# Block-diagonal 64-row products for groups 4 to 11 in a fused DeltaNet and gated-MLP kernel, with a re-planned order of work

## The chip, the cores and the metric

The kernel runs on one NeuronCore of a Trainium2 chip. The metric is the device time of one execution in microseconds (us). The kernel before takes 633.71 us in the median of 3 runs (633.09 to 634.2).

A core has a matrix engine (TensorE, PE in the profile, with weight loads as PEld), a vector engine (VectorE, DVE), a scalar engine (ScalarE, ACT), a general one (GpSimd, POOL) and one that issues transfers (SyncE, SP). Each works through its own instructions in order. TensorE writes to PSUM, which has eight banks of 2 KB per partition; the other engines copy from there to SBUF.

## The reference

Two parts follow each other. The first is a delta rule with a state per head (4 batches, 8 heads, 768 steps, head size 48):

```
k_n = k / (norm(k) + 1e-6)
for t in range(768):
    y[t]  = q[t] @ state
    v_old = k_n[t] @ state
    state = state + beta[t] * outer(k_n[t], v[t] - v_old)
```

The second is a gated MLP over the 3072 tokens of y (384 wide, 1536 hidden): `(sigmoid(x @ w_gate) * (x @ w_val)) @ w_out`. All in float32.

## The kernel before

**The recurrence in chunks.** The 768 steps are cut into 12 groups of 64 tokens. Within a group the recurrence becomes a triangular system: the updates u solve `(1/gamma + strictly lower part of K K^T) u = v - K state`. All 32 pairs of batch and head are done at once; a 64-token block is held as two 32-token halves that lie on different partitions. Per group g these steps run, named here as the planner names them:

- `gram`: K K^T of the keys (32 products of 48 rows, 64 records in the trace, since a float32 product leaves two). The diagonal 32x32 blocks are copied to `G` (line 258), the corner blocks between the two halves to `L` (line 262).
- `n`, `h`, `T`: norms and the inverse of the 32x32 triangular blocks on VectorE, for two groups together (`norms`, `solve`), with a transpose into `mt` at the end (line 310). Groups 0 and 1 take a shorter way: `solve_pair` inverts 16x16 blocks and `joining` (`pz`, `pm`, lines 366 and around) builds the 32x32 inverses with products.
- `pk` (`rest`, line 384): K state. `less` (line 393) subtracts it from v on VectorE.
- `u.0`, `u.1`, `u.2` (`updates`): the inverse times the first half (line 414), the corner block times that result, accumulated onto `pk` (line 407), then, after a second `less`, the inverse times the second half (line 414). `keep_u` (lines 420, 422) copies the results into `su`, a quarter of the partitions at a time, since heads of different kinds go to different places. In each 128-row operand four 32-row products lie beside each other.
- `pp` with `masked` (lines 273, 278): the masked q K^T. `yy` (`rows`, lines 442 and 445): the outputs. `pd` (`advance`, line 469) and `s` (line 478): the new state. `pt`, `xh`, `xl` (lines 500, 507, 509): the outputs transposed and split into a high and a low part for the MLP.

The chain from one group to the next is `pk`, `less`, `u.0`, copies, `u.1`, `less`, `u.2`, copies, `yy`, `pd`, `s`.

**The MLP in tiles.** Groups form units: 0 and 1 alone (256 tokens, "narrow"), then pairs (512 tokens, "wide"). A unit goes through 12 slices of the hidden width; each slice is a `gate`, a `val` and an `out` product of nine records each (lines 521 and 557; a narrow unit has gate and val in one step). float32 precision comes from splitting weights and inputs into two parts and making three products. In between run the sigmoid, the product and the split (lines 526, 531, 536, 541). Units 0 and 1 alternate in runs of slices (`RUNS`), because their weights arrive and are unpacked (lines 153 to 176) while they work.

**The order of work.** Nothing is ordered by hand: `schedule()` is a planner that runs when the kernel is built. Every step is a task with an engine, a cost in ns, the tasks it follows, and tokens it takes and gives back (`aux` for four PSUM banks, `mt`, `row` and others for buffers). For each engine the planner picks, among the tasks that can start soonest (within `SLACK`), the one with the highest level: the longest chain of costs behind it, plus `URGENCY` by name, plus `LIFTS` by group for the names in `FIRST` or `CHAIN`. The result is a fixed order for each engine. Up to the first product tile, gaps on TensorE are filled with `warm` products (line 185). The planner counts TensorE's instructions in pages of 256; `SHIFTS` tiny products ahead of `pz0` (line 191) move where the pages end.

Of the kernel before, what the change touches and what calls it, by code (L numbers as in the profile page):

```python
# [26 lines left out]
N = S // C  # L27
# [25 lines left out]
RUNS = {0: (0, 6, 12), 1: (0, 9, 12)}  # L53
EPS = 1e-6
EARLY, FLIGHT, HUSH = 3, 2, 6
QUIET = "pm0"
# [3 lines left out]
def deltanet_gated_mlp(ctx: ExitStack, tc: tile.TileContext, kd, qd, kv, beta, words, out):  # L60
# [13 lines left out]
    mt = const.tile([128, 2, CP, 32], F32, name="mt")  # L74
# [7 lines left out]
    scratch = wk.tile([128, 3, CP, 32], F32, name="scratch", tag="xa0", bufs=1)  # L82
# [22 lines left out]
    def load_rows(g, part):  # L105

        st = state[g]
        st["kv"[part]] = wk.tile([128, CP, D], F32, name=f"{'kv'[part]}_{g}", tag="kv"[part], bufs=2)
        pairs = [(st["kv"[part]].rearrange("p c d -> p (c d)"), kv[g, :, part * CP * D:(part + 1) * CP * D])]
        if part and g % 2 == 0:  # L110
            st["beta"] = wk.tile([128, 32], F32, name=f"beta_{g}", tag="beta", bufs=2)
            pairs.append((st["beta"], beta[:, g // 2]))
        move(pairs)

    def constants():
# [8 lines left out]
        state[0]["X"] = X = wk.tile([128, 1056], F32, name="X_0", tag="xa1", bufs=1)  # L124
        nc.gpsimd.memset(X, 0.0)
        nc.gpsimd.memset(scratch[:, 0], 0.0)
# [115 lines left out]
    def gram(g):  # L242
# [5 lines left out]
        st["L"] = L = wk.tile([128, CP, 32], F32, name=f"L_{g}", tag="L", bufs=2)  # L248
# [7 lines left out]
        def block(e, n):  # L256
            lo, hi, o = ((0, 128, 0), (32, 64, 32), (96, 128, 32))[n]
            (nc.vector.tensor_copy if g < 2 and e else nc.scalar.copy)(out=G[lo:hi, :, e * J:(e + 1) * J], in_=pg[e][lo:hi, :, o:o + 32].rearrange("q p t -> q t p"))  # L258

        def corner(e, t):  # L260
            lo, o = t + 32 * e, 32 - 32 * e
            nc.scalar.copy(L[lo:lo + 32, e * J:(e + 1) * J], pg[e][lo:lo + 32, :, o:o + 32])
# [25 lines left out]
    def solve(g):  # L288
# [21 lines left out]
        nc.vector.transpose(mt.rearrange("q g c i -> q i c g"), X.rearrange("q i (c g) -> q i c g", g=2))  # L310
        yield

    def lower_left(g):

        a = scratch[:, 0]
        nc.scalar.activation(a[:, :, 0:16].rearrange("q c t -> q t c"), state[0]["G"][:, 0:16, :, g], AF.Copy, scale=under)
# [28 lines left out]
    def flipped(g):  # L345

        nc.vector.transpose(scratch[:, 1].rearrange("q c t -> q (c t)"), mt[:, g].rearrange("q c t -> q (c t)"))
# [5 lines left out]
    def joining(g, n):  # L353
# [8 lines left out]
        lhsT, rhs = (scratch[:, 0], mt[:, g]) if n == "pz" else (scratch[:, 1], scratch[:, 2])  # L362
        out, rhs = out[:, :, 16:], rhs[:, :, 16:]
        for c in range(CP):
            for r in range(0, 128, 32):
                last = nc.tensor.matmul(out=out[r:r + 32, c], lhsT=lhsT[r:r + 32, c], rhs=rhs[r:r + 32, c], start=True, stop=True)
# [4 lines left out]
    def keep_z(g):  # L371

        nc.scalar.copy(scratch[:, 2, :, 16:], state[g]["pz"][:, :, 16:])


    def rest(g):
# [4 lines left out]
        for j in range(J):  # L381
            for e, x in KINDS:
                r, t = 64 * e, tokens_at(e, x)
                nc.tensor.matmul(out=pk[e][t:t + 64, j], lhsT=kq[r:r + D, x, j], rhs=su[r:r + D, 2 if x else e, j],  # L384
                                 start=j == 0, stop=True, skip_group_check=True)
        if g:
            st["R"] = [None, None]

    def less(g, e, step):
        st = state[g]  # L390
        if st["R"][e] is None:
            st["R"][e] = wk.tile([128, J, D], F32, name=f"R_{g}_{e}", tag="row", bufs=2)
        nc.vector.tensor_tensor(out=st["R"][e], in0=st["v"][:, e * J:(e + 1) * J], in1=st["pk"][e], op=ALU.subtract)  # L393

    def updates(g, step):

        st = state[g]
        if g == 0 and "R" not in st:
            st["R"] = [st["v"][:, e * J:(e + 1) * J] for e in range(2)]
        R, L = st["R"], st["L"]  # L400

        at = {(e, x): [tokens_at(e, x) + 32 * (k ^ e) for k in range(2)] for e, x in KINDS}
        if step == 1:
            for j in range(J):
                for e, x in KINDS:
                    one, two = at[e, x]
                    nc.tensor.matmul(out=st["pk"][e][two:two + 32, j], lhsT=L[one:one + 32, e * J + j], rhs=su[one:one + 32, 3 if x else e, j],  # L407
                                     start=False, stop=True, skip_group_check=True)
            return
        st["pu"] = pu = [ps_aux.tile([128, J, D], F32, name=f"pu_{g}_{step}_{x}", tag="aux") for x in range(1 if g else 2)]  # L410
        for j in range(J):
            for e, x in KINDS:
                r = at[e, x][step // 2]
                nc.tensor.matmul(out=pu[0 if g else x][r:r + 32, j], lhsT=mt[r:r + 32, g % 2, e * J + j], rhs=R[e][r:r + 32, j], start=True, stop=True)  # L414

    def keep_u(g, step, e, x):

        r, pu = tokens_at(e, x) + 32 * ((step // 2) ^ e), state[g]["pu"]
        if g == 0 and x:
            nc.vector.tensor_copy(out=su[r:r + 32, 3 if x else e], in_=pu[1][r:r + 32])  # L420
        else:
            nc.scalar.copy(su[r:r + 32, 3 if x else e], pu[0][r:r + 32])  # L422
# [168 lines left out]
    SHIFTS = 5  # L591
# [23 lines left out]
    pools = dict(flight=EARLY, aux=4, gv=1, po=2, G=1, gp=1, mt=2, scratch=1, row=2, ys=1, sg=2, h=2, u=2, L=2, xa=0, xb=1, mq=2)  # L615
# [422 lines left out]
```

## Time and profile before

| | |
|---|---|
| median of 3 runs | 633.71 us |
| profiled execution, whole | 636.26 us |
| its span, first to last instruction | 634.5 us |
| granted TensorE clock, mean | 0.991 |
| first product tile (`gate0`) starts | 50.62 us |
| TensorE busy | 617.0 us |
| VectorE busy | 393.7 us |
| ScalarE busy | 255.9 us |
| GpSimd busy | 10.0 us |

The groups of instructions name a line, an engine, an operation, what is written and read, the shape and the count, then busy time, mean length of one in ns, and the idle time ahead of it. In the timeline a row merges neighbours of one kind: start, length, engine, line, operation, shape, count, and in brackets the idle time before it and what ended that. Matmuls overlap, so the length of a row of them reaches past the start of the next row.

### The profile page before, as it was taken

Reading aid. Unit: us, or ns where it says so; the run is one execution under the profiler, and the core shown is the slowest. Engines: PE = TensorE matmul, PEld = TensorE weight load, DVE = VectorE, ACT = ScalarE, POOL = GpSimd, SP = SyncE. Lnnn points to the kernel's source line nnn. Section 1 sums busy time; section 2 is a strip of 40 time slices with the busy share of each in tenths; the row PEclk is TensorE's granted clock in tenths of the full one; section 3 lists DMA queues with packets and bytes.
Section 4 is the critical chain, followed back from the end, with each engine's and each line's share of the span. In section 5 each row is a group of like instructions: output and inputs, shape, how many; then the busy total and the mean of one; then the engine's idle time right before and its main releaser. Section 6 shows DMA issues by size and latency. Waiting matters only on the chain.

```text
span 634.5 us, 20716 instructions
## 1 busy us (share of the span) xinstructions
PE 617.0 (97%) x9372; PEld 502.4 (79%) x9381; DVE 393.7 (62%) x876; ACT 255.9 (40%) x506; POOL 10.0 (2%) x25
## 2 busy tenths in 40 slices
PE   8878999999999999999999999999999999999997
PEld 5457899989887777788787877778888777888886
DVE  4887779996699652499544499753399744212222
ACT  4477995264521234722224621235521143221212
POOL 3000000000000000000000000000000000000000
PEclk9978999999999999999999999999999999999999
DMA  8867663004210131020041130021130000010001
GB/s 220 263 167 219 190 189 96 2 28 113 61 50 26 27 110 38 2 74 5 23 112 28 35 101 2 26 66 48 35 101 1 1 3 3 2 51 0 1 1 50
DMA packets 16216, 40.75 MB, mean 64 GB/s; under 512 B 2944, under 2 KB 3968, under 8 KB 16128
## 3 DMA queue, kind: packets, MB, share of 16 engines
q1 hardware_dynamic: 15920, 39.10, 21.3%
q8 instruction: 73, 1.20, 0.8%
q10 hardware_dynamic: 208, 0.33, 0.1%
q14 instruction: 15, 0.12, 0.1%
HBM read 34.70 MB, written 4.72 MB: 62 GB/s over the span
## 4 chain that ended last, share of the span: by engine, by line
PE 87%; ACT 5%; DVE 5%; issue 1%; DMA 1%; SPq 0%; ACTq 0%
PE gv_g L521 26%; PE po L557 22%; PE gv_v L521 20%; PE pu L414 3%; PE warm L185 3%; PE pk L384 2%; PE pp L273 2%; PE yy L442 2%; PE pg L254 2%; PE yy L445 2%; ACT G L258 1%; PE pd L469 1%; PE pt L500 1%; PE pk L407 1%; ACT w L172 1%
## 5 line engine op out<-in xcount | busy, mean ns | idle before, releaser
L521 PE MATMUL gv_g<-x,w 128*128 128x512 f32 (+1 forms) x756 | 167.3, 368 | 0.7 <-DVE x L509 0.6
L557 PE MATMUL po<-h,w 128*128 128x512 f32 (+1 forms) x756 | 167.5, 366 | 0.3 <-DVE h L541 0.2
L557 PEld LDWEIGHTS po<-h,w 128*128 128x128 f32 x756 | 127.1, 188 | 25.1 <-DVE h L541 0.7
L521 PEld LDWEIGHTS gv_g<-x,w 128*128 128x128 f32 x756 | 126.7, 190 | 24.8 <-DVE x L509 0.9
L521 PE MATMUL gv_v<-x,w 128*128 128x512 f32 x540 | 136.9, 397 | 0.0
L521 PEld LDWEIGHTS gv_v<-x,w 128*128 128x128 f32 x540 | 99.9, 188 | 23.4
L536 ACT CAST h<-sg 128x512 fp32r<-128x512 f32 (+1 forms) x84 | 47.0, 559 | 144.0 <-DVE sg L531 139.7
L531 DVE TENSOR_TENSOR sg<-sg,gv_v 128x512 f32<-128x512 f32 x60 | 41.2, 687 | 97.9 <-PE gv_v L521 97.5
L526 ACT ACTIVATE sg<-gv_g 128x512 f32<-128x512 f32 (+1 forms) x84 | 45.0, 536 | 123.7 <-PE gv_g L521 123.4
L541 DVE TENSOR_TENSOR h<-sg,h 128x512 fp32r<-128x512 f32 (+1 forms) x84 | 51.4, 611 | 44.4 <-ACT h L536 43.9
L422 ACT COPY su<-pu 32x384 f32<-32x384 f32 x92 | 43.3, 470 | 51.8 <-PE pu L414 50.5
L305 DVE TENSOR_TENSOR tmp<-X,gp 128x31 f32<-128x31 f32 (+15 forms) x155 | 52.9, 341 | 4.1
L308 DVE TENSOR_TENSOR X<-X,tmp 128x31 f32<-128x31 f32 (+15 forms) x155 | 52.9, 342 | 3.8
L278 DVE TENSOR_TENSOR kqp<-pp,pmask 64x512 f32<-64x512 f32 x48 | 32.3, 686 | 7.6 <-PE pp L273 7.0
L478 DVE TENSOR_TENSOR su<-su,pd 48x384 f32<-48x384 f32 x40 | 22.0, 551 | 20.3 <-PE pd L469 19.6
L258 ACT COPY G<-pg 32x256 f32<-32x256 f32 (+1 forms) x66 | 26.0, 393 | 10.9 <-PE pg L254 9.5
L521 PE MATMUL gv_g<-xx,w 128*128 128x256 f32 x216 | 28.3, 285 | 0.7 <-DVE sg L531 0.7
L521 PEld LDWEIGHTS gv_g<-xx,w 128*128 128x128 f32 x216 | 26.6, 191 | 1.2 <-DVE sg L531 0.9
L185 PE MATMUL warm<-zero 128*128 128x512 bf16 x83 | 23.2, 430 | 2.4 <-issue 1.3
L393 DVE TENSOR_TENSOR R<-v,pk 128x384 f32<-128x384 f32 x44 | 22.3, 550 | 4.7 <-PE pk L384 4.2
L509 DVE TENSOR_TENSOR x<-pt,x 128x384 fp32r<-128x384 f32 x22 | 11.7, 554 | 19.9 <-ACT x L507 19.8
L414 PEld LDWEIGHTS pu<-R,mt 32*32 32x32 f32 x1408 | 16.6, 105 | 6.2 <-issue 5.1
(98 smaller groups left out, 482.8 us busy)
## 6 DMA issues: line engine op xcount, KB each, us to landing
raw<-in_words_dram SPq DMA_DIRECT2D x36, 384.0 KB, 3.8
kqp<-in_qd_dram SPq DMA_DIRECT2D x24, 256.0 KB, 4.0
v<-in_kv_dram SPq DMA_DIRECT2D x12, 384.0 KB, 4.0
k<-in_kv_dram SPq DMA_DIRECT2D x12, 384.0 KB, 3.5
kqp<-in_kd_dram SPq DMA_DIRECT2D x23, 192.0 KB, 3.5
out_dram<-ot SPq DMA_DIRECT2D x14, 256.0 KB, 2.0
out_dram<-ot SPq DMA_DIRECT2D x7, 128.0 KB, 1.7
kqp<-in_kd_dram ACTq DMA_DIRECT2D x1, 192.0 KB, 4.5
```

The source lines that it names most:

```text
L185: nc.tensor.matmul(out=hot[0], lhsT=z.to_broadcast([128, 128]), rhs=z.to_broadcast([128, 512]), start=True, stop=True)
L258: (nc.vector.tensor_copy if g < 2 and e else nc.scalar.copy)(out=G[lo:hi, :, e * J:(e + 1) * J], in_=pg[e][lo:hi, :, o:o + 32].rearrange(" ...
L305: nc.vector.tensor_tensor(out=tmp, in0=X[:, j:32, j:j + 1].to_broadcast([128, n, j]), in1=gp[:, j:j + 1, 0:j].to_broadcast([128, n, j]), o ...
L308: nc.vector.tensor_tensor(out=X[:, j:32, 0:j], in0=X[:, j:32, 0:j], in1=tmp, op=ALU.add)
L414: nc.tensor.matmul(out=pu[0 if g else x][r:r + 32, j], lhsT=mt[r:r + 32, g % 2, e * J + j], rhs=R[e][r:r + 32, j], start=True, stop=True)
L422: nc.scalar.copy(su[r:r + 32, 3 if x else e], pu[0][r:r + 32])
L521: nc.tensor.matmul(out=pg, lhsT=parts[w, f][:, a, k * 128:(k + 1) * 128], rhs=x[b][:, k], start=(k == 0 and q == 0), stop=(k == KC - 1 and ...
L526: nc.scalar.activation(h, st["g", f], AF.Sigmoid)
L531: nc.vector.tensor_tensor(out=h, in0=h, in1=st["v", f], op=ALU.mult)
L536: nc.scalar.copy(hh[:, 0], st["sg", f])
L541: nc.vector.tensor_tensor(out=hh[:, 1], in0=st["sg", f], in1=hh[:, 0].bitcast(F32), op=ALU.subtract)
L557: nc.tensor.matmul(out=po[k], lhsT=parts["o", f][:, w, k * 128:(k + 1) * 128], rhs=hh[:, a], start=begins(p, f) and q == 0 and (p > 1 or k ...
```

## The change

Six things change together.

- **Inverse as a block-diagonal operand (groups 4 to 11, `WIDE`).** `mt` becomes the front of a larger tile `both`, in which each 32-column inverse block has a second column block beside it. The solve's transpose `T` writes the blocks of all rows into column block 0; ScalarE copies those of the second and fourth quarter of the partitions to column block 1 (`aside`), and GpSimd clears them in column block 0 (`blank`). Two 32x32 blocks then stand on the diagonal of a 64x64 operand, and an update step is 16 products of 64 rows instead of 32 of 32 rows. So that both halves meet the right rows, v and beta are reordered on the way in for these groups, `less` takes 32-row quarters from alternating banks, and a second set of rows is gathered by four ScalarE copies (`gather`) and one subtraction.
- **64-row step between the halves (all groups).** ScalarE copies the whole bank of first-half results to `uc` (`keep_all`); `across` multiplies with corner blocks that stand off the diagonal of a zeroed 64x64 operand (`corner_of`), 16 products into a bank of its own (`pl`), and `less_first` subtracts that from the rows in place. The copies into `su` are no longer ahead of it. `rest` is left out for group 0, whose state is zero.
- **The first join (`pz`) with 64 rows**: `lower_left` runs as four quarter instructions into a block-diagonal operand, and 32 products take the place of 64.
- **Seven tiles of group 0 first** (`RUNS`), instead of six.
- **Small steps held back**: where TensorE's last task was a product tile and groups 4 on are concerned, a task counts as startable only `HOLDS` after it is ready (`pp` 24 us, `pt` 15, `gram` 1), unless nothing else is left.
- **Planner tables**: costs, `URGENCY`, `LIFTS`, `SLACK`-like limits, `SHIFTS` from 5 to 32, a charge of 180 ns for a small step that follows a product tile in place of a discount of 200 for one that follows a small step; and the key rows for the state have one buffer instead of two.

```diff
-RUNS = {0: (0, 6, 12), 1: (0, 9, 12)}
+RUNS = {0: (0, 7, 12), 1: (0, 9, 12)}
+WIDE = 4
...
+    both = const.tile([128, 2, 2, J, 2, 32], F32, name="both")
+    flat = both.rearrange("p g s j h i -> p (g s j h i)")
+    mt = flat[:, 0:2 * CP * 32].rearrange("p (g c i) -> p g c i", g=2, c=CP)
+    corner_of = [const.tile([128, J, 2, 32], F32, name=f"L{i}") for i in range(2)]
...
+        to = both[:, :, :, :, 0].rearrange("q g s j i -> q i (s j) g") if g >= WIDE else mt.rearrange("q g c i -> q i c g")
+        nc.vector.transpose(to, X.rearrange("q i (c g) -> q i c g", g=2))
...
+    def aside(q):
+        nc.scalar.copy(both[32 * q:32 * q + 32, :, :, :, 1], both[32 * q:32 * q + 32, :, :, :, 0])
+    def blank(q):
+        nc.gpsimd.memset(both[32 * q:32 * q + 32, :, :, :, 0], 0.0)
+    def lower_left(g, q):
+        mine = slice(32 * q, 32 * q + 32)
+        nc.scalar.activation(wide_a[mine, :, q % 2, 0:16].rearrange("q c t -> q t c"), state[0]["G"][mine, 0:16, :, g], AF.Copy, scale=under[mine])
...
         for c in range(CP):
-            for r in range(0, 128, 32):
-                last = nc.tensor.matmul(out=out[r:r + 32, c], lhsT=lhsT[r:r + 32, c], rhs=rhs[r:r + 32, c], start=True, stop=True)
+            if n == "pz":
+                for r in (0, 64):
+                    last = nc.tensor.matmul(out=out[r:r + 64, c], lhsT=wide_a[r:r + 64, c], rhs=mt[r:r + 64, g, c, 16:], start=True, stop=True)
...
+    def gather(g, q):
+        nc.scalar.copy(st["pc"][rows], st["pk"][1 ^ q % 2][rows])
...
+    def less(g, s, q=None):
+        rows = slice(0, 128) if q is None else slice(32 * q, 32 * q + 32)
+        r, st = halves_of(g)[rows, s], state[g]
+        nc.vector.tensor_tensor(out=r, in0=r, in1=st["pk"][s] if g < WIDE else st["pc"] if q is None else st["pk"][s ^ q % 2][rows], op=ALU.subtract)
+    def less_first(g, s):
+        r = halves_of(g)[:, s]
+        nc.vector.tensor_tensor(out=r, in0=r, in1=state[g]["pl"], op=ALU.subtract)
...
+            if g >= WIDE:
+                for r in (0, 64):
+                    nc.tensor.matmul(out=pu[0][r:r + 64, j], lhsT=both[r:r + 64, g % 2, s, j], rhs=R[r:r + 64, s, j], start=True, stop=True)
+                continue
...
+    def keep_all(g):
+        nc.scalar.copy(uc, state[g]["pu", 0][0])
+    def across(g):
+                nc.tensor.matmul(out=pl[r:r + 64, j], lhsT=corner_of[g % 2][r:r + 64, j], rhs=st["uc"][r:r + 64, j], start=True, stop=True)
...
-    SHIFTS = 5
+    SHIFTS = 32
...
+                if e == PE and not shape[0] and not filling:
+                    options = [o for o in options if o[0] >= when[o[1]["n"]] + HOLDS.get(o[1]["name"].rstrip("0123456789."), 0) or int(o[1]["name"].strip("abcdefghijklmnopqrstuvwxyzU").split(".")[0]) < 4] or options
...
-    LIFTS = {0: 100000, 1: 15000, 2: 0, 3: 15000}
+    LIFTS = {0: 60000, 1: 15000, 2: -5000, 3: 5000}
...
-    TURNED = 200
+    SWITCH = 180
+    HOLDS = dict(gram=1000, pp=24000, pt=15000, pk=0, pd=0)
```

More of the change, by code (lines that the diff above doesn't have):

```diff
@@ L416, in keep_u, with halves_of @@
[L416 to L422, printed above, removed]
+                nc.tensor.matmul(out=pk[e][t:t + 64, j], lhsT=kq[r:r + D, x, j], rhs=su[r:r + D, 2 if x else e, j], start=True, stop=True)
+    def halves_of(g):
+        return state[g]["v"].rearrange("p (s j) d -> p s j d", s=2)
@@ L746, in keeps @@
             return out
-        task(f"u{g}.0", PE, 810, lambda: updates(g, 0), r + [f"T{g if g < 2 else g - g % 2}"], take=("aux",) * (2 if two else 1))
-        k0 = keeps(0, [f"u{g}.0"])
-        task(f"u{g}.1", PE, 810, lambda: updates(g, 1), k0 + corners[g] + r, free=("L",))
-        l1 = [task(f"less{g}.1.{e}", DVE, 555, lambda e=e: less(g, e, 1), [f"u{g}.1"], free=("aux",)) for e in range(2)]
-        task(f"u{g}.2", PE, 810, lambda: updates(g, 2), l1, take=("aux",) * (2 if two else 1), free=("row", "row", "mt") if g else ("mt",))
@@ L752, in recurrence @@
-        k2 = keeps(2, [f"u{g}.2"])
-        task(f"yy{g}", PE, 2150, lambda: rows(g), k2 + m + was, take=("aux", "aux", "ys"))
+        word, pay = ("U", 600) if g >= WIDE else ("u", 812)
+        task(f"{word}{g}.0", PE, pay, lambda: updates(g, 0), r[:4] + ([f"T{g if g < 2 else g - g % 2}"] if g < WIDE else blanks[g - g % 2]), take=("aux",))
+        task(f"uc{g}", ACT, 472, lambda: keep_all(g), [f"{word}{g}.0"], take=("uc",))
+        k0 = keeps(0, [f"{word}{g}.0", f"uc{g}"])
+        task(f"a{g}", PE, 600, lambda: across(g), [f"uc{g}"] + corners[g], take=("aux",), free=("L", "uc"))
@@ L754, in recurrence @@
+        kind = (1,) if g >= WIDE else (0, 1)
+        l2 = [task(f"less{g}.2.{k}", DVE, 555, lambda k=k: less_first(g, k), [f"a{g}"] + r, free=("aux",) if k else ()) for k in kind]
+        task(f"{word}{g}.2", PE, pay, lambda: updates(g, 1), l2, take=("aux",) * (2 if two else 1), free=("mt",))
+        k2 = keeps(1, [f"{word}{g}.2"])
+        task(f"yy{g}", PE, 2147, lambda: rows(g), k0 + k2 + m + was, take=("aux", "aux", "ys"))
         yc = [task(f"y{g}.{e}", DVE if two and e else ACT, 560 if two and e else 480, lambda e=e: keep_y(g, e), [f"yy{g}"], free=("aux",)) for e in range(2)]
@@ L949, in schedule @@
                 small = t["name"][:3] not in ("gat", "val", "out")
-                cost -= TURNED if small and shape[0] else 0
+                cost += SWITCH if small and not shape[0] and not filling else 0
                 shape[0] = small
```

175 lines of the change are left out of this document (98 added, 77 removed), and 13 rows, old and new, of the table URGENCY.

## Prediction, made before the result was known

> **What bounds the kernel now.** I read the page's busy shares first, then the busy time by stretch, then the timeline of TensorE (its rows: start us, length us, engine, line, operation, tiles, shapes, count, idle time before).
>
> ```profile
> span 634.5 us, 20716 instructions
> ...
> PE 617.0 (97%) x9372; PEld 502.4 (79%) x9381; DVE 393.7 (62%) x876; ACT 255.9 (40%) x506; POOL 10.0 (2%) x25
> ```
> ```profile
> 32.00:48.00 16.00, 12.30 (x447) 9.36 (x453) 13.67 (x21) 11.85 (x19) 0.00 (x0) 0.79 0.63 172
> ...
> 172.00:545.00 373.00, 373.00 (x5460) 297.38 (x5461) 239.89 (x543) 128.34 (x258) 2.91 (x3) 1.00 0.14 39
> ```
>
> From 172 to 545 us TensorE (first figure after the stretch) is never idle, at a granted clock of 1.00; VectorE has work for 239.89 and ScalarE for 128.34 of those 373 us. There a saved TensorE microsecond is a saved microsecond of the span, and added work on the other engines costs nothing while it is not late. Before 50 us it is the other way round: from 32 to 48 us VectorE is busy for 13.67 of 16, and TensorE partly idles or runs `warm` fillers.
>
> Lengths of matmul rows overlap, so I take a step's cost from one row's start to the next row's start.
>
> ```profile
> 194.92 0.94 PE L469 MATMUL pd<-su,k 64*48 64x48 f32 x64
> ...
> 204.28 2.26 PE L521 MATMUL gv_v<-x,w 128*128 128x512 f32 x9
> 206.38 2.26 PE L557 MATMUL po<-h,w 128*128 128x512 f32 x9
> 208.57 1.15 PE L384 MATMUL pk<-su,kqp 48*64 48x48 f32 x64
> 209.65 2.36 PE L521 MATMUL gv_g<-x,w 128*128 128x512 f32 x9
> 211.85 2.26 PE L557 MATMUL po<-h,w 128*128 128x512 f32 x9
> ...
> 216.14 0.88 PE L414 MATMUL pu<-R,mt 32*32 32x48 f32 x64
> 216.95 2.35 PE L521 MATMUL gv_g<-x,w 128*128 128x512 f32 x9
> 219.23 0.88 PE L407 MATMUL pk<-su,L 32*32 32x48 f32 x64
> 220.04 2.35 PE L521 MATMUL gv_v<-x,w 128*128 128x512 f32 x9
> ...
> 226.55 1.15 PE L442 MATMUL yy<-su,kqp 48*64 48x48 f32 x64
> 227.63 1.14 PE L445 MATMUL yy<-su,kqp 128*64 128x48 f32 x32
> 228.70 2.36 PE L521 MATMUL gv_g<-x,w 128*128 128x512 f32 x9
> ...
> 542.00 0.82 PE L500 MATMUL pt<-ident,ys 128*128 128x128 f32 x6
> ```
>
> A 32-row step (`updates`, 32 products, 64 records) holds TensorE from 216.14 to 216.95, 0.81 us or 12.7 ns a record; the corner product on line 407 also 0.81. `rest` takes 1.08 for 64 records (16.9 ns), the first half of `rows` 1.08 for 64 (16.9), `advance` 0.86 for 64 records with 48 weight columns (13.4), and the full-height half of `rows` 1.07 for 32 (33.4 ns). A product tile of nine records takes 2.10 (204.28 to 206.38), but 2.19 ahead of a small step and 2.20 behind it: going into a burst of small steps and out of it costs 0.19.
>
> **The change part by part.** *The 64-row step.* For groups 4 to 11 each of the three update products becomes 16 products of 64 rows by 64 columns, 32 records; for groups 0 to 3 only the middle one does (`across`). The trace has no such step with this exact pattern. The nearest row is `rows` line 442 (64 columns of weights, 48 moving, half heights taken in turn): 32 records at 16.9 ns are 0.54 us. Bounds: 13.4 ns as in `advance`, 0.43; and 33.4 ns as in the full-height half, 1.07, if the two halves did not run beside each other. I take 0.54, a saving of 0.27 a step. Outside the startup there are 8 groups x 3 + 3 groups x 1 = 27 of them: **-7.3 us** (bounds -10.3 and +7.0).
>
> ```profile
> L414 PEld LDWEIGHTS pu<-R,mt 32*32 32x32 f32 x1408 | 16.6, 105 | 6.2 <-issue 5.1 <-ACT L L262 0.4
> ...
> L442 PEld LDWEIGHTS yy<-su,kqp 64*64 64x64 f32 (+1 forms) x736 | 12.0, 134 | 4.0 <-issue 2.5 <-ACT L L262 0.7 <-DVE su L420 0.4
> ```
>
> In the groups by line a load of 32 columns takes 105 ns and one of 64 columns 134: 1.28 times, not twice. The Trainium skill, "TensorE: Matmul & The Clock Gate", section on LDWEIGHTS, says that a weight load costs its columns divided by 1.2 ns and nothing for its rows. By that rule 32 loads of 64 columns are worth 64 loads of 32, and this term would be 0 instead of -7.3.
>
> *The pair of joins.* `pz` falls from 64 products to 32. Group 1's runs from 49.43 to 50.62 (rows below), 1.19; with 64 records at 16.9 ns it is 1.08: **-0.1**. Group 0's lies in the startup.
>
> *Holding back.* With `HOLDS`, the planner lets `pp` wait up to 24 us, `pt` 15 and `gram` 1 after they are ready, for groups 4 on, unless another small step has just opened a burst. From 194.92 to 542.00 (rows above, the first and the last) I count 60 bursts; 48 contain a step of the recurrence (`pk`, `pu`, `yy`, `pd`) and stay; 12 hold nothing but `pp`, `pt` or `gram`. If 8 of the 12 join another burst, 8 x 0.19 = **-1.5** (bounds 0 and -2.3).
>
> *Startup.* The first product tile starts at 50.62.
>
> ```profile
> 34.70 0.54 PE L414 MATMUL pu<-v,mt 32*32 32x48 f32 x15 [0.74 <-DVE mt L351]
> 36.17 1.19 PE L414 MATMUL pu<-v,mt 32*32 32x48 f32 x49 [0.93 <-issue]
> 37.70 1.06 PE L185 MATMUL warm<-zero 128*128 128x512 bf16 x2 [0.34 <-issue]
> 38.69 1.09 PE L407 MATMUL pk<-su,L 32*32 32x48 f32 x64
> ...
> 49.43 1.26 PE L366 MATMUL pz<-mt,scratch 32*32 32x16 f32 x128
> 50.62 2.37 PE L521 MATMUL gv_g<-x,w 128*128 128x256 f32 x18
> ...
> 54.43 0.68 PE L384 MATMUL pk<-su,kqp 48*64 48x48 f32 x31 [0.79 <-issue]
> ...
> 59.53 0.79 PE L366 MATMUL pm<-scratch 32*32 32x16 f32 x49 [1.35 <-issue]
> 60.25 3.65 PE L521 MATMUL gv_g<-x,w 128*128 128x256 f32 x18
> ```
> ```profile
> 31.48 2.71 DVE L278 TENSOR_TENSOR kqp<-pp,pmask 64x512 f32<-64x512 f32 x4
> 34.22 0.42 DVE L351 TENSOR_TENSOR mt<-mt,pz 128x256 f32<-128x256 f32 x1
> ```
> ```profile
> 34.71 0.78 ACT L316 ACTIVATE scratch<-G,under 128x256 f32<-128x256 f32 x1
> 35.55 0.83 ACT L172 CAST w<-u 128x768 fp32r<-128x768 f32 x1
> 37.39 0.96 ACT L422 COPY su<-pu 32x384 f32<-32x384 f32 x2 [1.01 <-PE pu L414]
> ```
>
> Now the corner product (38.69) waits for four copies of quarters, two on ScalarE (37.39 to 38.35) and two on VectorE; after, for one copy of the whole bank, half of ScalarE's 0.96: -0.5 us. The corner product itself halves in records, 1.09 to about 0.6 at that stretch's clock of 0.79: -0.5. The removed `rest` of group 0 and 27 more tiny `shift` products stand where fillers stand: 0. Against it, `lower_left` becomes four instructions of about 0.78 instead of one, twice, so 2 x 3 x 0.78 = 4.7 us more of ScalarE, of which group 1's 2.3 fall beside weight preparation; ScalarE has 4.1 us free between 32 and 48, and if that cover is gone the chain is up to 2.3 late. Waits for nothing the profile names ("issue") cut into steps: 0.93 here; and VectorE ran 2.71 us of masks right before the operation (34.22) that the chain waited for, at a priority that the new table changes. I take -1 for these two of a possible -3.6: startup **-2.0** (bounds +2.3 and -4.6).
>
> *Early product tiles.* Seven tiles of group 0 instead of six ahead of group 1's nine: the same tiles in another order, 0. The waits at 54.43 and 59.53 (0.79, 1.35) and the tile at 60.25 that took 3.65 where the same work took 2.37 at 50.62 (+1.28) may come back elsewhere: 0, bounds -3.4 and +3.
>
> ```profile
> q8 instruction: 73, 1.20, 0.8%
> ```
>
> These waits look like instruction fetches: 1.20 MB in 73 packets is 16 KB, about 256 of TensorE's 18,753 loads and products, each. The change removes some 2,100 of them (28 steps x 64, 128 of `rest`, 2 x 128 of `pz`, less 54 of `shift`), 8 packets. The Trainium skill, "Runtime: NRT & Kernel Launch", section on instruction fetch, calls crossing such a block mostly hidden, which would make every such term 0; the trace shows 0.8 to 1.4 us at the worst ones.
>
> *Other engines.*
>
> ```profile
> 213.22 2.02 DVE L310 STREAM_TRANSPOSE mt<-X 128x1024 f32<-128x1024 f32 x1
> ```
> ```profile
> 217.09 1.95 ACT L422 COPY su<-pu 32x384 f32<-32x384 f32 x4 [4.38 <-PE pu L414]
> ```
> ```profile
> L286 POOL MEMSET X<- 128x1024 f32 x5 | 4.8, 963 | 449.2 <-DVE gp L199 449.2
> ```
> ```profile
> 357.12 1.02 DVE L509 TENSOR_TENSOR x<-pt,x 128x384 fp32r<-128x384 f32 x2 [3.36 <-ACT x L507]
> ```
> ```profile
> 364.15 1.10 PE L521 MATMUL gv_g<-x,w 128*128 128x512 f32 x4
> ```
>
> Between the transpose that ends a pair's solve (213.22 to 215.24) and the first update (216.14) now stand two ScalarE copies of 1,024 elements (estimated from 0.83 for 768: 1.1 each) and a GpSimd clear (0.96): about 3.2 us later, once a pair. Each group's chain has two more subtractions (half of 1.02 each) ahead of its first update and four gathering copies (1.95) beside it, but one copy instead of four (-1.46) and one subtraction less behind it: about even. Work queued behind them on ScalarE (the product tiles' sigmoid and split) moves by half a microsecond at a time. What hides all this is the slack at the end of a pair: the fourth wide unit's inputs are ready at 358.14 and its first tile starts at 364.15, 6.0 us later. If the chain slips by more, TensorE idles at that border. I take **0**.
>
> Sum: -7.3 - 0.1 - 1.5 - 2.0 = **-10.9 us**. The profiled execution took 636.26 (span 634.5, 1.76 around it), 2.55 above the median 633.71. I take the sum off both: span 623.6, median **622.8**.
>
> **Rivals.**
> 1. *Held transposes meet the border.* A pair's last `pt` may wait 15 us, the slack is 6.0. If it is released only when the unit's tiles run out, TensorE idles for transposes, copy and subtraction, about 2 us, at four borders: +8, 630.8. For: 542.00 is a burst of that kind, with nothing behind it to join. Against: the following pair's `gram` opens a burst there.
> 2. *The startup keeps its length and fetch waits land on its chain*: the -2.0 is lost and another 2.7 come: 627.5. For: the three larger "issue" rows above lie inside steps of 64 and 128 records. Against: fewer instructions.
> 3. *Weight columns set the price*: the steps save nothing: 633.7 - 0.1 - 1.5 - 2.0 = 630.1. Against: 105 and 134 ns. It is the page's rule above.
> 4. *Slower: the two 64-row halves take turns*, so a record costs 33.4 ns as at full height and a step 1.07: 27 x 0.26 = +7.0, with the other terms 637.1. It decides from 25.3 ns a record (0.81 / 32) on. For: each new product comes back to the same quarter of the array every second time. Against: lines 384 and 442 alternate halves at 16.9.
> 5. *The change doesn't do what it says*: the replanned order opens as many new bursts and idle gaps as the steps save: 633 to 635.
>
> **How the numbers follow.** Forecast 0.60, rival 1 0.10, 2 0.12, 3 0.05, 4 0.06, 5 0.04, and 0.03 for a gain beyond the bounds I kept (under 618). A measurement tells 0.2%, 1.3 us, from no change. Faster: 0.60 + 0.10 + 0.12 + 0.05 + 0.03 = 0.90; the same 0.04; slower 0.06. The range 618 to 631 holds the forecast and rivals 1 to 3; the forecast's own is 618 to 627.
>
> **What would show it.** Right: in groups 4 to 11 three steps of 32 records with 64x64 weights, 0.54 us from start to start; about 52 bursts where there were 60; TensorE without idle time from 172 us on; the first product tile near 48.6; about 65 instruction packets. Wrong: 64-row steps of 0.8 us or more; a product tile that waits for `x` at a unit's border; more "issue" time before 80 us.

## The result and the profile after

The changed kernel takes 641.44 us in the median (641.12 to 643.37, 4 runs), the kernel before beside it 633.85. The ratio of the means is 1.0128, with a 95% interval of [1.0105, 1.015]; below, the number with brackets behind each time is this ratio to the kernel before. The forecast was 622.8 in a range of 618 to 631. The change made the kernel 7.6 us slower.

The page of the changed kernel (span, busy time by engine, transfers of instructions):

```profile
span 639.2 us, 18692 instructions
...
PE 619.8 (97%) x8299; PEld 508.4 (80%) x8307; DVE 402.8 (63%) x892; ACT 287.1 (45%) x564; POOL 20.8 (3%) x37
...
q8 instruction: 65, 1.06, 0.7%
```

TensorE has 1,073 matmul records fewer than before and is busy 2.8 us longer. Its share is still 97%, so this is where the time is. The timeline of TensorE in the wide part (columns as in the prediction):

```profile
220.89 1.14 PE L442 MATMUL pu<-v,both 64*64 64x48 f32 x32
221.95 2.35 PE L599 MATMUL po<-h,w 128*128 128x512 f32 x9
...
246.43 1.13 PE L459 MATMUL pl<-uc,L 64*64 64x48 f32 x32
247.50 2.35 PE L563 MATMUL gv_g<-x,w 128*128 128x512 f32 x9
249.78 1.14 PE L442 MATMUL pu<-v,both 64*64 64x48 f32 x32
250.84 2.35 PE L563 MATMUL gv_v<-x,w 128*128 128x512 f32 x9
```

The step that was to take 0.54 us from start to start takes 1.06 (220.89 to 221.95, 249.78 to 250.84), the corner product 1.07 (246.43 to 247.50): 33 ns a record. With half as many records the step is 0.25 longer than the 0.81 of before.

To see how the 7.6 us divide, take the start of the first wide tile and of the last 18 records of `out`, first in the kernel before, then in the changed one:

```profile
170.75 0.50 PE L521 MATMUL gv_g<-x,w 128*128 128x512 f32 x1
...
626.60 4.36 PE L557 MATMUL po<-h,w 128*128 128x512 f32 x18
```
```profile
171.38 0.50 PE L563 MATMUL gv_g<-x,w 128*128 128x512 f32 x1
...
631.25 4.36 PE L599 MATMUL po<-h,w 128*128 128x512 f32 x18
```

Before, that stretch is 455.85 us; after, 459.87. **The wide part lost 4.0 us.** To the end of those records it is 460.2 and 464.2, the figure that I call "the wide part" for every kernel below. The rest of the 7.6, some 3 to 3.6, was lost ahead of 171 us. The profiled execution of before is one of its longer ones there: two experiments that share its startup (the blocks of test products below) reached the first wide tile at 169.42 and 168.32.

The startup of the changed kernel on TensorE, up to its first product tile:

```profile
34.86 1.50 PE L446 MATMUL pu<-v,both 32*32 32x48 f32 x64 [1.25 <-DVE both L375]
37.18 1.95 PE L459 MATMUL pl<-uc,L 64*64 64x48 f32 x32 [0.82 <-ACT uc L451]
...
48.29 1.87 PE L390 MATMUL pz<-both,scratch 64*64 64x16 f32 x58 [0.18 <-DVE x L551]
...
54.00 0.78 PE L393 MATMUL pm<-X,scratch 32*32 32x16 f32 x58 [2.01 <-issue]
...
57.93 1.49 PE L446 MATMUL pu<-v,both 32*32 32x48 f32 x60 [0.94 <-issue]
59.35 3.23 PE L563 MATMUL gv_g<-x,w 128*128 128x256 f32 x18
```

The chain of group 0 is where it was (first update at 34.86 against 34.70). But the first product tile starts at 59.35 instead of 50.62: the whole of group 1's join, the first update and two "issue" waits (2.01 and 0.94) now stand ahead of it. And the granted clock is lower. The busy time by stretch (PE, PEld, DVE, ACT, POOL, then PEclk), after and then before:

```profile
28.00:44.00 16.00, 10.95 (x361) 7.93 (x363) 14.04 (x22) 13.86 (x21) 0.00 (x0) 0.68 0.63 196
...
53.00:65.00 12.00, 10.06 (x248) 9.41 (x249) 10.87 (x16) 9.79 (x16) 0.00 (x0) 0.72 0.66 184
...
172.00:545.00 373.00, 372.61 (x4668) 299.43 (x4669) 248.38 (x557) 152.88 (x303) 10.53 (x11) 1.00 0.14 40
```
```profile
28.00:44.00 16.00, 11.40 (x491) 8.20 (x497) 13.95 (x21) 10.81 (x17) 0.00 (x0) 0.79 0.66 195
...
53.00:65.00 12.00, 9.86 (x295) 9.28 (x296) 8.70 (x15) 7.57 (x14) 0.00 (x0) 0.86 0.69 201
```

By these means TensorE lost (1 - 0.68) x 16 + (1 - 0.72) x 12 = 8.5 us of clock, against 5.0 before. From 172 us on, TensorE idles for 0.4 us of 373, as foreseen: the loss there is work, not waiting.

### The profile page after: what moved, and what is told of

Same layout as the page of the kernel before. It is cut to its first block, busy times and chain, and to the rows that moved or that the text cites. A ratio compares the mean times of both kernels' runs of the same rounds, so it can differ in the third digit from the quotient of the medians.

```text
span 639.2 us, 18692 instructions
## 1 busy us (share of the span) xinstructions
PE 619.8 (97%) x8299; PEld 508.4 (80%) x8307; DVE 402.8 (63%) x892; ACT 287.1 (45%) x564; POOL 20.8 (3%) x37
## 3 DMA queue, kind: packets, MB, share of 16 engines
q8 instruction: 65, 1.06, 0.7%
HBM read 34.70 MB, written 4.72 MB: 62 GB/s over the span
## 4 chain that ended last, share of the span: by engine, by line
PE 86%; DVE 3%; ACT 2%; issue 1%; DMA 1%; ACTq 0%; DVEq 0%
PE gv_g L563 27%; PE po L599 23%; PE gv_v L563 20%; PE pu L442 3%; PE pk L411 2%; PE pp L284 2%; PE pl L459 2%; PE yy L484 2%; PE yy L487 2%; PE pg L264 1%; PE pt L542 1%; PE pd L511 1%; PE pu L446 1%; ACT su L464 1%; DMA out_dram<-ot 1%
## 5 line engine op out<-in xcount | busy, mean ns | idle before, releaser
L269 ACT COPY G<-pg 32x256 f32<-32x256 f32 (+1 forms) x66 | 23.4, 397 | 9.5 <-PE pg L264 8.7
L195 PE MATMUL warm<-zero 128*128 128x512 bf16 x71 | 21.4, 454 | 2.1 <-issue 1.0
L428 DVE TENSOR_TENSOR v<-v,pk 32x384 f32<-32x384 f32 (+1 forms) x38 | 20.7, 551 | 3.2 <-PE pk L411 2.8
L433 DVE TENSOR_TENSOR v<-v,pl 128x384 f32<-128x384 f32 x16 | 8.5, 552 | 21.6 <-PE pl L459 21.6
```

## The experiments

**What sets the price of a 64-row product.** Two kernels run the kernel before, and then a block of small products between fillers. The block's results are read by nobody; its time adds to the whole (702.86 and 663.7 us, one run each).

```diff
+            for j in range(J):           # two quarters on the diagonal, one bank (L1004)
+                for r in (0, 64):
+                    nc.tensor.matmul(out=banks[0][r:r + 64, j], lhsT=w[r:r + 64, 64 * j:64 * j + 64], rhs=x[r:r + 64, j], start=True, stop=True)
...
+                    nc.tensor.matmul(out=banks[2 + r // 64][abs(r - j % 2 * 64):abs(r - j % 2 * 64) + 64, j], ...)   # four quarters (L1012)
...
+                nc.tensor.matmul(out=banks[0][0:64, j % J], lhsT=w[0:64, ...], rhs=x[0:64, j % J], ...)   # one quarter (L1019)
```

> The kernel before with a block of float32 products behind its last tile, on data that lie in SBUF, apart from each other by fillers; the outputs of the block are read by nobody, so its whole time says nothing. Nine patterns of 32 records (16 products), each on its own line, all done twice; ns per record. Theory A1 (a quarter of the array that holds a 64-column product is taken for about 133 ns, so the rate follows from how many quarters are in rotation): two diagonal quarters into one bank (line 1004) 33, the same into two banks (1008) 33, four quarters in rotation (1012) 17, two row halves into the same column half (1016) 33, one quarter alone (1019) 66, two diagonal quarters with 16 moving columns (1023) 25 to 33, with 32 weight columns (1027) 25, four diagonal 32-row tiles (1031) 13, two of them (1035) 25. Theory A2 (two row halves that write one PSUM bank take turns): line 1004 33 and line 1008 17, line 1016 17. Theory A3 (the weight load of 64 rows is what is slow): all 64-row lines 33, line 1012 too.

The timeline of TensorE in the block (the fillers' start ends each):

```profile
632.19 1.14 PE L1004 MATMUL probe<-su 64*64 64x48 f32 x32
633.26 2.80 PE L185 MATMUL filler<-zero 128*128 128x512 bf16 x12
...
639.78 0.68 PE L1012 MATMUL probe<-su 64*64 64x48 f32 x32
640.39 2.80 PE L185 MATMUL filler<-zero 128*128 128x512 bf16 x12
...
646.91 2.06 PE L1019 MATMUL probe<-su 64*64 64x48 f32 x32
648.91 2.80 PE L185 MATMUL filler<-zero 128*128 128x512 bf16 x12
651.63 1.11 PE L1023 MATMUL probe<-su 64*64 64x16 f32 x32
652.67 2.80 PE L185 MATMUL filler<-zero 128*128 128x512 bf16 x12
```

The same 16 products take 2.00 us on one quarter of the array, 1.07 on two, 0.61 on four. By this a product of 64 weight columns holds its quarter for about 130 ns (2.00 / 16 = 125 on one; 2 x 1.07 / 16 = 134 on two; the longer steps on lines 384 and 442, which use four, give 4 x 2 x 16.9 = 135, the short block here 4 x 0.61 / 16 = 152), and what counts is how many quarters take turns. With 16 moving columns instead of 48 it is 1.04, so the moving columns hardly matter. Two banks (1.06) and two row halves into one column half (1.07, still two quarters) change nothing, so the halves do not collide in a bank; and the same 64 rows on four quarters take 0.61, so it is not the rows. With 32 weight columns, two tiles take 0.80 for 16 products, with 64 rows or 32, and four take 0.82 for 32 products.

The second block asked whether 32-row products can be made faster by more tiles in rotation.

> The kernel before with another block of 32-row, 32-column float32 products behind its last tile, outputs read by nobody. Theory A1 (a tile of the array is taken for about 100 ns by a 32-column product, and the rate follows from how many tiles are in rotation): four diagonal tiles 0.80 us for 32 products (line 1004), eight tiles in rotation with two banks about 0.4 (line 1009), two tiles 0.80 for 16 products (1013), one tile 1.60 for 16 (1016). If instead 12.7 ns a record is the rate at which TensorE takes instructions, line 1009 is 0.80 as well.

```profile
631.18 0.88 PE L1004 MATMUL probe<-su 32*32 32x48 f32 x64
632.23 2.57 PE L185 MATMUL filler<-zero 128*128 128x512 bf16 x11 [0.16 <-issue]
...
634.73 0.80 PE L1009 MATMUL probe<-su 32*32 32x48 f32 x64
635.69 2.57 PE L185 MATMUL filler<-zero 128*128 128x512 bf16 x11 [0.16 <-issue]
...
638.19 0.87 PE L1013 MATMUL probe<-su 32*32 32x48 f32 x32
638.99 2.79 PE L185 MATMUL filler<-zero 128*128 128x512 bf16 x11
641.71 1.54 PE L1016 MATMUL probe<-su 32*32 32x48 f32 x32
643.19 2.80 PE L185 MATMUL filler<-zero 128*128 128x512 bf16 x12
```

16 products of 32 columns take 1.48 on one tile (93 ns each) and 0.80 on two. 32 products take 1.05 to the next filler on four tiles (L1004) and 0.96 on eight (L1009), with a wait of 0.16 behind both: 0.89 and 0.80 without it, a tenth less and not half. So from four tiles on, at some 25 ns a product, more tiles hardly help. The 32-row step of before (0.81 for 32 products) is already there with its four tiles; the 64-row step, with two, is at 67 ns a product.

**The steps back to 32 rows, with the order unchanged.** The planner does not see the edit, so all engines keep the order of the changed kernel.

```diff
-                for r in (0, 64):
-                    nc.tensor.matmul(out=pu[0][r:r + 64, j], lhsT=both[r:r + 64, g % 2, s, j], rhs=R[r:r + 64, s, j], start=True, stop=True)
+                for r in (64, 32, 0, 96):
+                    nc.tensor.matmul(out=pu[0][r:r + 32, j], lhsT=both[r:r + 32, g % 2, s, j, r // 32 % 2], rhs=R[r:r + 32, s, j], start=True, stop=True)
```

This is the edit for the two update products of groups 4 to 11; the corner product of all groups is edited in the same way in the second kernel, and both in the third.

> The changed kernel with the planner's order kept and only the two inverse products of groups 4 to 11 (16 steps) made of 32 products of 32 rows again, from the same diagonal blocks; nothing is left out of the computation. Theory A (two 64-row halves take turns): a step goes from 1.06 to 0.81 us, 16 x 0.25 = 4.0 us less than the changed kernel, about 637.4. Theory B (the loss is in the startup and in the longer chains on ScalarE, VectorE and GpSimd): within 1 us of 641.4.

> The changed kernel with the planner's order kept and only the corner product of all groups made of 32 products of 32 rows again (into its own bank as in the change); nothing is left out. Theory A: 11 steps outside the startup x 0.25 = 2.8 us less, about 638.7, and the startup about as long. Theory B: within 1 us of 641.4.

> Both of these together: no 64-row product is left in the updates, the rest of the change stays. Theory A: 27 x 0.25 = 6.8 us less, about 634.7, no different from the kernel before by more than 1.5 us. Theory B: still about 641. If it is clearly below 633 the held-back small steps and the new order are worth something by themselves.

Measured, in this order: 638.63 us, 1.0065 [1.0041, 1.009]; 641.35, 1.0113 [1.0095, 1.0131]; 636.68, 1.0038 [1.0018, 1.0059]. The second is as slow as the changed kernel, where 638.7 was expected: its first wide tile starts at 174.07, 2.7 later, which takes back what its wide part wins. So the wide part is the better measure; in all three kernels TensorE is busy for the whole 369.0 us from 176 to 545. Timeline of the third:

```profile
224.39 0.88 PE L442 MATMUL pu<-v,both 32*32 32x48 f32 x64
225.21 2.35 PE L600 MATMUL po<-h,w 128*128 128x512 f32 x9
227.49 0.88 PE L460 MATMUL pl<-uc,L 32*32 32x48 f32 x64
228.30 1.16 PE L284 MATMUL pp<-kqp 48*64 48x64 f32 x64
```

Twice the records, and 0.82 and 0.81 instead of 1.06. The wide part is 460.89, 461.81 and 458.88 us against 464.23: 3.3, 2.4 and 5.35 less, for 16, 8 and 24 steps of a quarter microsecond. Without the 64-row steps the wide part is 1.3 better than before. **Shown: the 64-row steps cost 5.35 us.** But the third kernel as a whole is still slower than before, so some 3.6 to 4.1 us (2.3 to 2.8 more in all, and the 1.3) are lost ahead of the wide part.

**Holding small steps back**, alone in the kernel before, and then taken away from the third kernel above:

```diff
+                if e == PE and not shape[0] and not filling:
+                    options = [o for o in options if o[0] >= when[o[1]["n"]] + HOLDS.get(...) or int(...) < 4] or options
+                    soon = min(a for a, _ in options)
...
+    HOLDS = dict(gram=1000, pp=24000, pt=15000)
```

> The kernel before with the hold-back rule alone (gram 1 us, pp 24, pt 15, groups 4 on); nothing left out. Theory A (a burst of small steps costs 0.19 us to enter and leave, and the rule makes 53 of 60 of them): 7 x 0.19 = 1.3 us less, about 633 where the kernel before has 634.3, and 458.9 us instead of 460.2 from the first wide tile to the last. Rival: the held transposes come too late at a unit's border, and it is the same or up to 8 us slower.

638.76 us, 1.0082 [1.006, 1.0104]: alone it makes the kernel before slower, and the loss is in the wide part (464.5 against 460.2). The timeline at a unit's border:

```profile
359.28 2.37 PE L557 MATMUL po<-h,w 128*128 128x512 f32 x9
361.58 0.94 PE L469 MATMUL pd<-su,k 64*48 64x48 f32 x64
362.44 0.55 PE L500 MATMUL pt<-ident,ys 128*128 128x128 f32 x3
364.34 0.55 PE L500 MATMUL pt<-ident,ys 128*128 128x128 f32 x3 [1.35 <-DVE x L509]
```

The transposes of the next unit wait until its tiles run out, and TensorE then stands at the border for VectorE: rival 1's mechanism, seen in this kernel at this one border, with 1.6 us of idle time (1.35, and 0.24 for `pp` behind it). Another 2.1 us are lost a few tiles further on, at 375.09, where a tile waits for VectorE (the waits of TensorE: us in total, times, the longest):

```profile
PE gv_v L521 <- DVE sg L531: 2.1, 1, 2.1
```

No other border between wide units has idle time. In the changed kernel the border at the same place has none either.

```diff
-    HOLDS = dict(gram=1000, pp=24000, pt=15000, pk=0, pd=0)
+    HOLDS = {}
```

> e3 with the hold-back rule taken out and the rest of the new tables kept; nothing left out. Theory A: about 7 bursts more from the first wide tile on, 7 x 0.19 = 1.3 us more there (460.2 instead of 458.9), the early part as in e3. Rival: with these tables the rule does nothing, both within 0.4 us.

637.81, 1.0049 [1.0026, 1.0073]; the wide part is 459.30 with 57 bursts, against 458.88 with 53. There, holding back is worth 0.4 us.

**The place of the first product tiles.** The 59.35 above suggested that the late first tile costs the early time. Two kernels move tiles within the kernel before (the first one only after group 1's first update; seven tiles of group 0 alone), one re-plans the third kernel with three tiles lifted, two move `gate0` and `gate1` earlier in an order that is kept otherwise (changed kernel; third kernel).

```diff
-        ready = [f"wlo{number[f, 'gv']}"] + xs + ...
+        ready = ["u1.0"] * (i == 0) + [f"wlo{number[f, 'gv']}"] + xs + ...
```
```diff
-RUNS = {0: (0, 6, 12), 1: (0, 9, 12)}
+RUNS = {0: (0, 7, 12), 1: (0, 9, 12)}
```
```diff
+            if t["name"] in ("gate0", "gate1", "gate2"):
+                t["lift"] = 1000000
```
```diff
-    for t in schedule():
+    plan = schedule()
+    by_start = {t["name"]: t for t in plan}
+    by_start["gate0"]["start"] = by_start["pk1"]["start"] - 0.1
+    by_start["gate1"]["start"] = by_start["pm1"]["start"] - 0.1
+    for t in sorted(plan, key=lambda t: t["start"]):
```

> The kernel before with one dependency more: the first tile of group 0 after group 1's first update, the order that the changed kernel has there; nothing left out. Theory C: 2 to 4 us slower than the kernel before, all of it ahead of the first wide tile, with more issue waits and half clock between 48 and 66 us. Rival D: within 1 us.

> The kernel before with seven tiles of group 0 first instead of six; nothing left out. The prediction's term for it was 0: within 1.5 us of the kernel before, from the first wide tile on within 0.5.

> The changed kernel without 64-row products in the updates (as in e3) and with the first three tiles of group 0 put ahead of everything else once they are ready, as they stood in the kernel before; nothing left out. Theory C (the rest of the loss is that 11 us of group 1's small steps stand in one piece ahead of the first tile, with fetch waits and the half clock inside): the first wide tile starts some 3 us earlier than in e3, the time falls from 636.7 to about 633.5. Rival D (the early loss is ScalarE's added lower_left and copies, or the seven tiles): within 1 us of 636.7.

> The changed kernel, its planned order kept as it is but for two tiles: gate0 moved to just ahead of pk1 and gate1 to just ahead of pm1, where the kernel before has them; nothing left out. Theory C (fetch waits and half clock in 11 us of small steps without a tile between them cost 2 to 4 us): the first wide tile starts 2 to 4 us earlier, about 638.5. Rival D (what is lost early is lost in the steps themselves and in their waits on ScalarE and VectorE, wherever the tiles stand): within 1 us of 641.4.

> The same two tiles moved, without 64-row products in the updates (as in e3). Theory C: about 634, 2 to 4 less than e3's 636.7. Rival D: within 1 us of 636.7.

Measured: the late tile 652.04, 1.0286 [1.026, 1.0313]; seven tiles 644.3, 1.0168 [1.0141, 1.0195]; the third kernel with tiles lifted 637.1, 1.0053 [1.0031, 1.0074]; the changed kernel with two tiles moved 645.04, 1.0158 [1.0131, 1.0186]; the third with the same two moved 638.8, 1.0071 [1.0049, 1.0093]. In the three kernels with the tile put back to 50 to 52 us nothing was won; moving the two tiles made the changed kernel 3.6 worse and the third 2.1, more than either theory allowed. So putting the late first tile back does not bring the early time back. The late tile in the kernel before did cost 18 us, but its plan changed further on (22.6 us of small steps in one piece at 163.67), so it says little. Seven tiles first, in the kernel before, cost 10.6 us, all ahead of the wide part (its first wide tile starts at 176.53, its wide part takes 460.1). The three longest waits of TensorE in that kernel (us in total, times, the longest):

```profile
PE gv_g L521 <- DVE sg L531: 4.7, 1, 4.7
PE pu L414 <- DVE mt L351: 4.1, 1, 4.1
PE pm L366 <- ACT scratch L373: 3.0, 1, 3.0
```

The tiles are the same, but the plan around them is not; in the changed kernel, whose other edits are there too, the waits are other ones. What this edit is worth within the change stays open.

**The join.** `pz` with 64 rows takes longer than with 32 (58 ns a product at half the count), and `lower_left` in four pieces fills ScalarE. One kernel takes `pz` back to 32 rows, one takes `lower_left` back to one instruction as well, one does that in the third kernel.

```diff
-                for r in (0, 64):
-                    last = nc.tensor.matmul(out=out[r:r + 64, c], lhsT=wide_a[r:r + 64, c], rhs=mt[r:r + 64, g, c, 16:], start=True, stop=True)
+                for r in range(0, 128, 32):
+                    last = nc.tensor.matmul(out=out[r:r + 32, c], lhsT=wide_a[r:r + 32, c, r // 32 % 2], rhs=mt[r:r + 32, g, c, 16:], start=True, stop=True)
```

> The changed kernel, order kept, with the first join's 32 products of 64 rows made of 64 products of 32 rows again, lower_left still in four pieces; nothing left out. Theory A for this step (two tiles in rotation, at 16 moving columns as slow): pz of group 1 goes from 1.8 to 1.2 us, 0.6 to 0.8 less ahead of the first wide tile, about 640.7. Rival: no change.

> The same and lower_left as one instruction again in place of four (the three freed places in ScalarE's order stay empty); nothing left out. Theory E (ScalarE's added work, 4.4 us in lower_left, holds up group 0's and group 1's chain ahead of the first tiles): another 1.5 to 2.5 less, about 638.5. Rival F (what is left of the early loss is the new planned order itself): as e13.

> No 64-row product anywhere and lower_left in one piece, the changed kernel's order and the rest of the change kept; nothing left out. Theories A and E together: 636.7 - 0.7 - 2 = about 634, like the kernel before. Rival F: about 636.

In this order: 642.08, 1.0136 [1.0115, 1.0157]; 641.54, 1.0134 [1.0111, 1.0156]; 638.02, 1.0062 [1.0045, 1.0079]. No gain in any, so neither the join's products nor ScalarE's four pieces are seen to hold the early loss. But these edits add products ahead of the tiles, so that instruction fetches fall elsewhere too, and the next experiment shows that this alone can be worth more than the 0.7 to 2.5 us looked for.

**Where the instruction fetches fall.** The number of tiny `shift` products ahead of everything moves the places where TensorE's instruction blocks end, and no order changes: 5 instead of 32 in the last kernel, 64 instead of 32 in the changed one. Beside the second the changed kernel itself ran once more.

```diff
-        for _ in range(SHIFTS):
+        for _ in range(5):
```

> The same with 5 tiny shift products emitted where the plan has 32, so that every later fetch falls 54 instructions elsewhere; nothing left out. If the early loss is where the fetches fall, it moves by 1 to 3 us either way ahead of the first wide tile; if not, within 1 us of e15. From the first wide tile on, the same within 0.5.

> The changed kernel as it is, for a second profile of its early part beside the others. Theory A: 464.2 us from the first wide tile to the last, within 0.2. The first wide tile at 171 to 174; if it lies at 168 to 169, the early loss is scatter and not the change's.

> The changed kernel, order kept, with 64 tiny shift products emitted where the plan has 32: every later instruction fetch falls 64 instructions earlier in the steps; nothing left out. Theory G (where fetches fall decides 2 to 4 us ahead of the first wide tile): the time moves by over 1.5 us from the changed kernel's, up or down, and the longest issue waits lie at other steps. Rival: within 1 us of it. From the first wide tile on within 0.5 of 464.2.

642.17 us, 1.0132 [1.0105, 1.0159], which is 4.2 above the same kernel with 32; the changed kernel again 641.86 (638.97 to 646.27), 1.0125 [1.0088, 1.0162]; with 64, 640.23 (637.27 to 641.08), 1.009 [1.0063, 1.0116]. The kernel with 5 was to be within 0.5 of the one with 32 from the first wide tile on, and was not: its wide part is 462.0, against 459.35 with 32. Most of these 2.7 us are two waits of TensorE inside update steps, at 231.78 and 352.32 and at full clock; the kernel with 32 has none there:

```profile
PE pu L442 <- issue: 2.3, 2, 1.4
```

The intervals of the last two overlap, so 64 against 32 shows no difference. 5 against 32 does: 27 products more or less move the time by more than most edits of this change. Differences of a few us in the whole time are therefore weak evidence for any one edit here; the wide part without such waits is stronger.

**What the early loss goes with.** In the changed kernel's second profile the wide part is the same (464.15), while the first wide tile starts at 175.32 instead of 171.38, later than the 171 to 174 expected. What differs most is the clock. Busy time by stretch of that profile:

```profile
28.00:44.00 16.00, 9.75 (x309) 7.16 (x311) 12.50 (x19) 12.53 (x19) 0.00 (x0) 0.57 0.66 199
...
53.00:65.00 12.00, 9.32 (x266) 8.63 (x256) 10.97 (x15) 9.13 (x15) 0.00 (x0) 0.57 0.70 202
```

In all profiles the granted clock is either 1.00 or 0.50, and from 44 us on it is halved for about 3.4, 6.8, 10.2 or 13.7 us at a time. Ahead of each halving stands a stretch in which TensorE was not busy all the time. In the changed kernel, the stretch with the 2.01 "issue" wait and the one behind it; then the experiment that only holds steps back in the kernel before, whose largest "issue" wait there is 0.86:

```profile
51.00:54.40 3.40, 1.39 (x130) 1.24 (x126) 3.31 (x6) 3.21 (x5) 0.00 (x0) 1.00 0.76 214
54.40:61.20 6.80, 5.86 (x168) 5.40 (x157) 6.62 (x10) 5.54 (x9) 0.00 (x0) 0.50 0.61 186
```
```profile
44.00:82.00 38.00, 34.37 (x1049) 31.34 (x1046) 30.25 (x45) 34.64 (x63) 0.00 (x0) 1.00 0.72 197
```

TensorE was busy for 1.39 of 3.40 us, and then had half the clock for 6.8. Of the 13 profiles that I read for this, the three in which TensorE waits nowhere for as much as 1 us between 44 and 70 us (this one and the two with test products, all with the startup of before) have no halving there. In the others I found 14 halvings that begin between 44 and 172 us; in the 3.4 us ahead TensorE was busy for 0.5 to 2.3 us in twelve of them, and for 2.7 and 2.95 in two. The reverse does not hold: in the experiment of the last row TensorE was busy for 2.19 of the 3.40 us from 74.0 to 77.4, and the clock stayed at 1.00. So no threshold follows from these traces. The Trainium skill, "TensorE: Matmul & The Clock Gate", Part 1 on the clock gate, gives a free-running window of about 3.4 us and half the clock after an idle window. The lengths seen here agree; that the window must be idle does not, since it was busy for 41% in the row above and more in others.

The clock lost is (1 - mean granted clock) x span. Its median is 5.1 us over 65 executions of the kernel before and 11.2 over ten of the changed one. Among those ten, an execution with 1 us more of lost clock has a span 0.66 us longer (0.46 over all kernels and 161 executions). So the 6.1 us more of lost clock are worth 6.1 x 0.46 = 2.8 to 6.1 x 0.66 = 4.0 us; the early loss is 3 to 3.6. This is a relation seen over many executions, not an edit that put the clock back alone, and I have no run that did. One profile speaks against the clock as the whole cause: the changed kernel with 64 shift products lost 8.3 us of clock, about as much as the changed kernel's first profile (8.9), and yet its first wide tile starts at 169.13, where the kernels with the startup of before have theirs. That the clock causes the early loss is not shown.

## Why the prediction was wrong

- **The steps (-7.3 predicted): the step that failed.** The wide part shows +5.35 for 24 steps; with the three steps of groups 1 to 3 at the same 0.25, +6. The sentence that was wrong is "The nearest row is `rows` line 442". I matched the row by its shape (64 weight columns, 48 moving, row halves alternating) and not by how many quarters of the array take turns. Lines 384 and 442 pair each row half with both column halves, four quarters; the block-diagonal operand uses the two quarters on its diagonal and nothing else. The full-height half on line 445, two column halves in turn, was the row with the right number: 1.07 predicted as the far bound, 1.06 measured. Rival 4 had the mechanism ("each new product comes back to the same quarter of the array every second time"), the price of 1.07 a step and the point of 25.3 ns. It got a chance of 0.06 because of "lines 384 and 442 alternate halves at 16.9", which has no bearing: alternating halves was not the condition. It gave 637.1; 641.44 was measured. From -7.3 to +5.35 or +6 this term makes up some 13 of the 18.6 us between forecast and measurement.
- **Rival 3**, steps that save nothing because weight columns set the price, falls: a step costs 1.06, not 0.81. The 134 ns of a load is the length of its record and no rate: the same 32 loads of 64 columns go by in 2.00 us on one quarter (62 ns each) and in 0.61 us on four.
- **The joins (-0.1)**: the same error. Group 1's `pz` went from 1.19 to about 1.9 us (48.29 to 50.16, in a stretch at full clock), +0.7. Undoing it showed no gain, but that edit moves fetches too, so what it is worth stays open.
- **Holding back (-1.5)**: from 172 us on I count 53 bursts for 60, as foreseen (52), 7 x 0.19 = -1.3 by the prediction's price. The direct test, with 32-row steps, gave 0.4 for four bursts (0.8 by that price). Without the rest of the change the rule costs 4.3: 1.6 by rival 1's mechanism at one border, 2.1 in the wait behind it, the rest without a row. In the changed kernel TensorE doesn't idle at a border.
- **Sum of the wide part**: 24 x 0.25 = +6.0, less 1.3, is +4.7; +4.0 was measured. The 0.7 lies in the steps, which cost 5.35 / 24 = 0.22 each in the wide part where their rows say 0.25; why stays open. The -1.3 with 32-row steps agrees with the price of the bursts by luck: the direct test gives holding back 0.4 of it, and 0.9 belongs to the rest of the new order.
- **Startup (-2.0) and early tiles (0)**: wrong in sign together, some +3 to +3.6. I used the clock of 0.79 to scale durations, but gave its change no price of its own: the term "it may come back elsewhere: 0, bounds -3.4 and +3" took the waits for instructions as plain waits. The traces show what a wait of 1 to 2 us often has behind it, a halved clock for 3.4 to 13.7 us; the changed kernel lost 8.3 to 15.5 us of clock in its ten executions, the kernel before 1.9 to 10.8 with a median of 5.1. Rival 2 ("fetch waits land on its chain") pointed at the places of the fetches, which do move the time (5 against 32 shift products), but its price was too small, and TensorE waited no longer in all: 6.8 us of "issue" from 26 to 172 us before, 6.7 after. Moved tiles, `pz` and ScalarE's pieces brought nothing when undone.
- **Other engines (0)**: right. TensorE idles for 0.4 us between 172 and 545, with ScalarE busy 24.5 us longer there and GpSimd 7.6.
- **Instruction packets**: 65 foreseen, 65 measured. Fewer packets did not mean less waiting (the 6.8 and 6.7 above).

What stays open: which of the planner's edits moved the fetches and the small steps so, why the clock is halved for longer, and how much of the early loss is the clock's; the value of seven tiles within the change; 0.7 us of the wide part. No version that I ran is faster than the kernel before; the nearest is the third, 1.0038 [1.0018, 1.0059].

## What to carry to other kernels

Cost a small product by the tile of the array that it occupies: count how many different tiles take turns in the loop, and take the duration from a row with that count, not from one with the same shape. Merging products into larger block-diagonal ones halves the records and also halves the tiles in rotation; here four tiles of 32 were already near the shortest time that more tiles reach (25 ns a product), and two of 64 were not (67 ns). In a startup made of small steps, look at the granted clock by stretch before and after, because a halved clock often stands behind a wait of a microsecond or two, and by the relation above (0.46 to 0.66 us for each us of lost clock) 6.8 us at half clock go with 1.6 to 2.2 us.

## What the runs showed of the hardware that I had not expected

- A float32 product with 64 weight columns holds its quarter of the array for 125 to 134 ns with 16 or with 48 moving columns; one with 32 columns holds its tile for 93 to 100. Four 32-row tiles in turn reach 25 ns a product, and eight are only a tenth faster.
- The clock halved behind stretches of 3.4 us in which TensorE was busy for 0.5 to 2.3 us (twice 2.7 and 2.95), and stayed halved for 3.4, 6.8, 10.2 or 13.7 us; behind one with 2.19 it did not halve.
- 27 tiny products fewer ahead of the steps made the program 4.2 us slower (642.17 against 638.02); 2.3 us of it are waits for nothing the profile names, inside two steps of the wide part.
